# Another written-out order of steps, with casts, copies and state writes moved between engines, in a retention-plus-MLP kernel

## The chip, the core and the metric

The kernel runs on one core of one Trainium2 chip. A core has five engines, each of which works through its own instruction stream in order: TensorE (PE in the profile, with its weight loads as PEld), VectorE (DVE), ScalarE (ACT), GpSimd (POOL) and SyncE (SP). Here SP only issues DMAs, and POOL issues DMAs beside its arithmetic. The metric is the time of the whole program in device microseconds (us). Before the change it is 296.88 us, the median of three runs (296.61 to 297.04).

## The reference, cut to what matters

```python
q, k, v: (8 batches, 8 heads, 576 tokens, 64), float32; w_in (512, 2048); w_out (2048, 512)

scores = q @ k.transpose(0, 1, 3, 2) / sqrt(64)
gamma  = 1 - 2 ** (-5 - head)
Dmat   = gamma ** (row - col) where row >= col, else 0       # a decaying causal mask
x      = ((scores * Dmat) @ v), heads side by side           # (4608 tokens, 512)
h      = x @ w_in
g      = 0.5 * h * (1 + tanh(sqrt(2 / pi) * (h + 0.044715 * h ** 3)))
out    = g @ w_out                                           # (4608, 512)
```

## The kernel before, in words

**Retention.** A batch of 576 tokens is cut into five units: four of 128 tokens and a tail of 64. Units are numbered through, u = 0 to 39; u % 5 = 4 is a tail. Units 0, 2, 5 and 7 stand for two units each ("wide", 256 tokens). The decay is folded into the casts: `q` and `v` are multiplied by powers of gamma while they are cast from float32 to float16, and a running state of 64 by 64 per head carries the past. `L,u,n` loads q, k or v (n = 0, 1, 2) of unit u into one of seven pages of float32 (three from unit 31 on). `q,u`, `k,u`, `v,u` cast; the letter at the end names the engine (v VectorE, g GpSimd, a ScalarE). `D,u` transposes q and k of a unit by one DMA on SP; the first units are transposed on TensorE instead (`t`, copied out by `y`). `B,u,w` is a unit's TensorE work: the scores and the state products of unit u, and the output of unit w, the one before. Wide units have `X`, `Y` and `R` for that. `m,u` masks the scores, `a,u,half` and `o` update the state, `z,u,half` writes it as float16, `x,w` writes the output to xT, the left operand of the MLP. B has one buffer for scores and one for outputs, so the next B needs `m` and `a` of the last unit, and `x` of the one before, to be done.

**MLP.** Tokens go in nine blocks t of 512. For blocks 0 to 5, `N,t,fc,part` multiplies 256 tokens by 256 columns of w_in (eight matmuls), and `F` applies gelu. For blocks 6 to 8 the same product is made in four groups g of seven smaller products each (`A,t,g,i`, four matmuls) from sums of weights (`U`) and sums of xT (`s`); `l` combines them and `f` applies gelu. The second product is plain in block 0 and in the end of block 8 (`O`, four matmuls of 512 columns, copied out by `e`; `P` for the last rows, copied out by `E`). In between it is made in pairs of 128 rows by seven products (`W,t,pr,i`, eight matmuls) from sums of weights (`T`) and sums of gelu outputs (`H`); `V` combines the results, and `S` stores them (`Q` for the last rows). N, A and P share two PSUM banks, and so do O and W.

**Order.** Nothing is scheduled by a planner at run time. `ORDER` lists 1,332 steps, and each engine gets its instructions in the order of that list; the engines wait for each other by semaphores only. What a step is next to in the list means something only on its own engine. A step that waits holds up what stands behind it on that engine: a `D` on SP waits for its two casts, an `S` for its result, and the loads behind them wait too.

**Weights.** `I,g` (w_in) and `J,g` (w_out), eight each, are DMAs that GpSimd issues and that cast on the way; `N` with fc = 0 and 2 needs I,0 and I,1, fc = 4 and 6 needs I,2 and I,3, fc = 8 and 10 needs I,4 and I,5, fc = 12 and 14 needs I,6 and I,7. `O` of part p (the second number modulo 4) needs J,2p and J,2p+1. The steps `i` and `j` do nothing here, since all weights are loaded that way. `K,n` issues n matmuls whose result is not used, to fill TensorE's time before the first work. `w` loads the table of gelu, `c`, `g` and `Z` write constants and zeros.

Lines of the profile: 198 and 203 (wide loads), 215 and 221 (loads; 221 tails), 238 (weights), 269 and 267 (copies and casts on VectorE or GpSimd, and on ScalarE), 424 and 439 (q and v casts, wide ones), 483 (`D`), 529, 553, 563, 574 (`B`), 757 (`N`), 765 (`F`), 775 (`S`), 783 (`O`), 817 (`T`, `H`, `V`, `U`, `s`, `l` as sums), 860 (`W`), 957 (`A`), 987 (`P`), 1003 (`K`).

Of the kernel before, what the change touches and what calls it, by code (L numbers as in the profile page):

```python
# [17 lines left out]
L,0,1 Z,1,v L,0,0 I,2,g L,0,2 L,2,1 L,2,0 Z,2,g q,0 k,0,g I,7,g K,4 K,4 K,4 K,3 K,4 t,0,q,h L,2,2  # L18
L,4,1 c t,0,k,h I,1,g v,0,v X,0 y,0,k,v I,0,g I,3,g a,0,1 y,0,q,v Z,3,v k,2,g K,4 K,1 Y,0,1 t,2,k,o
m,0,1 z,0,1,a I,6,g K,4 Y,0,0 a,1,1 q,2 L,4,0 K,4 t,2,q,h m,0,0 y,2,k,a y,2,q,v I,4,g K,1 R,0 I,5,g  # L20
x,0 Y,2,1 L,5,0 x,1 i,4,v K,3 N,0,2,0 N,0,0,0 g o,1,1 m,2,1 L,5,1 Z,4,g v,2,v F,0,2,0 N,0,12,0 Y,2,0
F,0,0,0 z,1,1,v N,0,4,0 L,5,2 X,2 k,4,g Z,5,v q,4 F,0,12,0 F,0,4,0 t,4,k,o a,2,1 t,4,q,o a,3,1
y,4,q,a N,0,8,0 L,4,2 z,2,1,g L,9,1 N,0,10,0 F,0,8,0 k,5,g m,2,0 L,7,1 R,2 F,0,10,0 y,4,k,v B,4,-1
q,5 x,3 x,2 N,0,14,0 L,7,0 t,5,q,o N,0,0,1 L,7,2 J,1,g F,0,14,0 N,0,6,0 y,5,q,v J,3,g t,5,k,o
F,0,0,1 m,4 j,1,v J,0,g L,9,0 v,5,v J,2,g L,9,2 F,0,6,0 N,0,8,1 L,10,0 N,0,12,1 k,7,v X,5 y,5,k,a
F,0,8,1 z,3,1,g F,0,12,1 v,4,v Y,5,0 a,5,1 m,5,0 a,6,1 N,0,4,1 N,0,6,1 F,0,4,1 q,7 F,0,6,1 t,7,k,o
y,7,k,a N,0,2,1 J,5,g J,4,g N,0,14,1 F,0,2,1 J,6,g L,10,2 B,-1,4 F,0,14,1 x,4 Y,5,1 t,7,q,h y,7,q,a
J,7,g m,5,1 N,0,10,1 v,7,v F,0,10,1 z,5,1,g R,5 x,5 Y,7,0 o,6,1 x,6 O,0,0 O,0,4 q,10,g L,11,1
N,1,4,0 O,0,5 N,1,14,0 F,1,4,0 m,7,0 N,1,2,0 L,12,2 O,0,1 X,7 Y,7,1 F,1,14,0 F,1,2,0 L,15,1 k,9,a
O,0,6 O,0,2 N,1,10,0 F,1,10,0 q,9,g O,0,3 L,11,2 N,1,6,0 D,9 F,1,6,0 m,7,1 Z,0,g k,11,a a,7,1 O,0,7  # L30
e,0,0,v a,8,1 z,6,1,v O,0,12 T,1,0,v N,1,0,0 e,0,1,a F,1,0,0 z,8,1,g z,7,1,v N,1,8,0 O,0,13 L,10,1
N,1,12,0 R,7 B,9,-1 H,1,0,3,v v,10,v F,1,8,0 x,8 O,0,8 L,11,0 L,12,1 O,0,14 j,5,v F,1,12,0 v,11,v
T,1,1,v q,11 k,10,g x,7 O,0,15 N,1,6,1 H,1,0,1,v L,12,0 D,10 N,1,8,1 O,0,9 F,1,6,1 T,2,0,v v,9,v
O,0,10 e,0,3,a T,3,0,v S,0,0 N,1,14,1 F,1,8,1 H,1,0,2,v m,9 L,14,1 B,10,9 k,12,a D,11 T,2,1,v O,0,11
a,10,0 a,10,1 e,0,2,v N,1,12,1 L,13,2 F,1,14,1 L,13,0 x,9 N,1,10,1 m,10 F,1,12,1 T,3,1,v z,10,0,g
B,11,10 q,12,g W,1,0,1 S,0,3 v,13,v a,11,0 V,1,0,0,a a,11,1 x,10 v,12,v W,1,0,6 L,14,0 F,1,10,1
N,1,2,1 o,11,1 q,13,g F,1,2,1 T,4,0,v D,12 W,1,0,2 L,16,1 V,1,0,1,v N,1,4,1 N,1,0,1 S,0,2 V,1,0,2,a
z,11,0,v F,1,4,1 z,10,1,g j,2,v m,11 S,0,1 N,2,0,0 B,12,11 q,14 a,12,0 H,1,0,4,v k,15,g F,1,0,1
F,2,0,0 W,1,0,7 L,15,0 L,14,2 N,2,8,0 T,4,1,v N,2,4,0 V,1,0,3,v H,1,1,1,v L,13,1 z,12,0,g x,11
k,16,g H,1,1,2,v W,1,0,4 W,1,0,5 F,2,8,0 L,17,0 a,12,1 N,2,6,0 L,17,1 V,1,0,5,v L,19,0 F,2,4,0  # L40
k,13,g D,13 V,1,0,4,v F,2,6,0 m,12 N,2,14,0 v,14,v F,2,14,0 W,1,1,1 z,11,1,g V,1,1,0,a W,1,0,3
V,1,0,6,v L,16,0 N,2,10,0 F,2,10,0 k,14,g W,1,1,6 V,1,1,1,v N,2,12,0 z,12,1,v L,16,2 B,13,12 x,12
L,15,2 v,15,g D,14 q,15 W,1,1,2 H,1,1,3,v m,13 N,2,2,1 V,1,1,2,a W,1,1,7 F,2,12,0 N,2,2,0 V,1,1,3,v
k,17,a W,1,1,4 W,1,1,5 a,13,0 a,13,1 S,1,0 z,13,0,a q,19 q,17 q,16 F,2,2,1 S,1,1 D,15 L,17,2 F,2,2,0
L,18,0 N,2,8,1 B,14,13 N,2,12,1 L,20,0 F,2,8,1 V,1,1,5,v F,2,12,1 N,2,6,1 V,1,1,4,v W,2,0,1 x,13
N,2,10,1 F,2,6,1 m,14 H,2,0,1,v H,2,0,2,v z,13,1,v N,2,0,1 D,16 V,2,0,0,a L,24,1 B,15,14 H,1,1,4,v
a,15,0 L,18,2 H,2,0,3,v W,1,1,3 a,15,1 F,2,0,1 m,15 V,1,1,6,v q,18,g v,17,v F,2,10,1 N,2,4,1
N,2,14,1 L,18,1 L,19,1 x,14 v,16,g F,2,14,1 W,2,0,2 z,15,0,g B,16,15 W,2,0,6 F,2,4,1 x,15 k,19,g
a,16,0 N,3,8,0 V,2,0,1,v V,2,0,2,a a,16,1 F,3,8,0 o,16,1 z,16,0,v m,16 W,2,0,7 D,17 V,2,0,3,v L,23,1
v,18,g N,3,10,0 k,18,g F,3,10,0 L,24,0 L,20,1 N,3,4,0 F,3,4,0 z,15,1,g W,2,0,4 z,16,1,v B,17,16  # L50
L,21,0 N,3,0,0 q,20 V,2,0,5,v a,17,0 L,25,1 L,19,2 D,18 H,2,0,4,v L,20,2 S,1,2 W,2,0,5 N,3,12,0
W,2,1,1 F,3,0,0 m,17 q,21,g H,2,1,3,v V,2,0,4,v H,2,1,1,v F,3,12,0 k,20,g W,2,0,3 N,3,14,0 N,3,6,0
S,1,3 F,3,14,0 V,2,0,6,v V,2,1,0,a L,22,1 N,3,2,0 L,21,1 D,19 H,2,1,2,v W,2,1,6 a,17,1 x,16 z,17,0,g
# [73 lines left out]
def kernel(  # L127
# [11 lines left out]
    B, H, S, D = q.shape  # L139
# [239 lines left out]
    for h in range(H):  # L379
        pp, m = divmod(h, 4)  # L380
# [363 lines left out]
    gTs, h = {}, {}  # L744
# [331 lines left out]
```

## Time and profile before

| | us |
|---|---|
| median of three runs | 296.88 (296.61 to 297.04) |
| profiled execution: span from the first to the last instruction | 293.9 |
| profiled execution: its own time apart from the span | not given by the page |
| median less span | 3.0 |
| TensorE busy in the span | 280.3 (95%) |
| VectorE, ScalarE, GpSimd busy | 216.6, 150.1, 109.6 |
| first `N` starts | 21.3 |
| TensorE's last matmul group starts (32 matmuls, 2.65 us) | 288.2 |
| DMAs moved | 49.79 MB; HBM read 36.70 MB, written 9.44 MB |

The granted TensorE clock is full in all 40 slices. A busy TensorE says little by itself, since matmuls overlap and their ends are modelled; so it is read by the spacing of their starts: eight matmuls of 256 columns follow each other in 0.87 us (109 ns each), four of 512 columns in 0.86 us. By this pace the steps of the list can be laid out on a scale of TensorE work, counted from the first `N`: N and W are 0.87 us each, A 0.44, O 0.86, B 0.3 to 0.8. Positions such as "+20.9" below are this count, and "lead" is the distance of two steps on it.

### The profile page before, as it was taken

The page shows a single profiled execution, that of the slowest core. Times are in us where ns is not written, and L with a number is a line of the kernel's source. Part 1 is how long each engine was busy: PE and PEld are TensorE (multiplying, and loading weights), DVE is VectorE, ACT ScalarE, POOL GpSimd, SP SyncE. Part 2 cuts the span into 40 slices and gives each one's busy share as a digit, 9 for nine tenths or more (in the row PEclk, how much of TensorE's full clock was granted, in tenths as well). Part 3 has the DMA queues.
Part 4 walks back from the last instruction along what each step waited for, and adds up shares of the span by engine and source line. Part 5 has one row for each costly group of instructions (what it writes and reads, how often), then busy time and mean ns, then how long its engine had stood idle before and what let it go on. Part 6 is the DMA issues. An engine that isn't in the chain of part 4 may idle for free.

```text
span 293.9 us, 9639 instructions
## 1 busy us (share of the span) xinstructions
PE 280.3 (95%) x4064; PEld 235.2 (80%) x4064; DVE 216.6 (74%) x447; ACT 150.1 (51%) x289; POOL 109.6 (37%) x168
## 2 busy tenths in 40 slices
PE   3797999999999999999999999999999999999995
PEld 1355886667888888888888888888888788888874
DVE  7686753696865678576678699799889988977740
ACT  2144774334634543554553646546777587665411
POOL 5931910414351084163415544783467123000000
PEclk9999999999999999999999999999999999999999
DMA  7999999997979999989099978899498370002103
GB/s 212 283 236 250 217 220 211 214 179 162 248 142 228 178 186 220 230 206 210 23 235 214 196 166 178 187 204 153 131 195 208 75 205 7 36 8 102 74 25 121
DMA packets 136428, 49.79 MB, mean 169 GB/s; under 512 B 118208, under 2 KB 130880, under 8 KB 136384
## 3 DMA queue, kind: packets, MB, share of 16 engines
q1 hardware_dynamic: 132032, 44.97, 71.3%
q0 software_dynamic: 4352, 4.20, 8.5%
q8 instruction: 32, 0.52, 0.8%
q14 instruction: 12, 0.10, 0.1%
HBM read 36.70 MB, written 9.44 MB: 157 GB/s over the span
## 4 chain that ended last, share of the span: by engine, by line
PE 86%; POOL 5%; DMA 4%; DVE 3%; issue 1%; ACT 0%; POOLq 0%; ACTq 0%
PE bank L860 30%; PE bank L757 27%; PE bank L957 12%; PE bank L783 6%; DMA w_in_sb<-in_moe_w_in_dram 4%; PE sk L553 2%; PE x L529 2%; POOL w_in_sb L238 2%; PE sk L563 1%; PE x L574 1%; PE bank L987 1%; DVE pages L817 1%; POOL wide L269 1%; PE bank L493 1%; PE x L677 1%
## 5 line engine op out<-in xcount | busy, mean ns | idle before, releaser
L757 PE MATMUL bank<-xT,w_in_sb 128*128 128x256 f16 x768 | 94.4, 273 | 2.1 <-DMA w_in_sb<-in_moe_w_in_dram 2.1
L765 ACT ACTIVATE gT<-bank 128x512 f16<-128x512 f32 x96 | 56.7, 598 | 61.5 <-PE bank L757 59.7
L757 PEld LDWEIGHTS <-w_in_sb 128*128 128x128 f16 x768 | 73.8, 98 | 13.7 <-DMA w_in_sb<-in_moe_w_in_dram 2.7
L860 PEld LDWEIGHTS <-ssum 128*128 128x128 f16 x480 | 46.3, 98 | 6.5 <-issue 0.8
L269 POOL CAST sz<-s 64x256 f16<-64x256 f32 x48 | 24.4, 509 | 66.2 <-DVE s L713 45.9
L860 PE MATMUL bank<-tsum,ssum 128*128 128x256 f16 x360 | 46.0, 273 | 0.6 <-DVE ost L817 0.6
L860 PEld LDWEIGHTS <-gT 128*128 128x128 f16 x360 | 34.8, 98 | 4.5 <-issue 0.2
L424 POOL TENSOR_TENSOR qk<-pages,dec 128x512 f16<-128x512 f32 (+1 forms) x20 | 22.2, 1122 | 32.9 <-DMA pages<-in_q_dram 17.2
L860 PE MATMUL bank<-w_out_sb,gT 128*128 128x256 f16 x240 | 31.1, 273 | 0.0
L817 DVE TENSOR_TENSOR ssum<-gT 128x1024 f16<-128x1024 f16 x30 | 23.9, 798 | 3.9 <-ACT gT L765 3.5
L424 POOL TENSOR_TENSOR v<-pages,dec 128x512 f16<-128x512 f32 (+1 forms) x20 | 20.6, 1030 | 15.3 <-DMA pages<-in_v_dram 10.4
L817 DVE TENSOR_TENSOR ost<-u,bank 128x256 f32<-128x256 f32 x45 | 18.1, 416 | 9.5 <-PE bank L860 9.4
L817 DVE TENSOR_TENSOR ssum<-gT,ssum 128x1024 f16<-128x1024 f16 x30 | 23.4, 782 | 0.2
L691 DVE TENSOR_TENSOR ret<-sk,mask 128x512 f16<-128x512 f32 (+1 forms) x32 | 19.8, 618 | 4.3 <-PE sk L563 4.0
L957 PEld LDWEIGHTS <-pages 128*128 128x128 f16 x192 | 18.4, 98 | 2.8 <-issue 0.3
L957 PE MATMUL bank<-pages 128*128 128x256 f16 x144 | 20.3, 273 | 0.3 <-ACT pages L267 0.3
L783 PE MATMUL bank<-w_out_sb,gT 128*128 128x512 f16 x80 | 19.1, 380 | 0.0
L817 DVE TENSOR_TENSOR u<-u,bank 128x256 f32<-128x256 f32 x30 | 12.4, 415 | 8.7 <-PE bank L860 5.0
L713 DVE TENSOR_TENSOR s<-s,sk 128x256 f32<-128x256 f32 x36 | 14.9, 415 | 5.0 <-PE sk L563 4.0
L593 ACT ACTIVATE xT<-x 128x512 f16<-128x512 f32 (+1 forms) x25 | 14.3, 578 | 8.0 <-PE x L574 8.0
L817 DVE TENSOR_TENSOR hc<-hc,bank 128x512 f32<-128x512 f32 x21 | 14.4, 684 | 5.0 <-PE bank L957 2.3
L267 ACT COPY hc<-bank 128x512 f32<-128x512 f32 x19 | 11.1, 585 | 12.5 <-PE bank L957 12.4
(114 smaller groups left out, 425.8 us busy)
## 6 DMA issues: line engine op xcount, KB each, us to landing
out_dram<-ost SPq DMA_DIRECT2D x35, 256.0 KB, 3.4
pages<-in_q_dram SPq DMA_DIRECT2D x32, 256.0 KB, 4.7
pages<-in_v_dram SPq DMA_DIRECT2D x24, 256.0 KB, 4.1
pages<-in_k_dram SPq DMA_DIRECT2D x24, 256.0 KB, 4.3
pages<-in_k_dram SPq DMA_DIRECT2D x4, 512.0 KB, 5.2
pages<-in_v_dram SPq DMA_DIRECT2D x4, 512.0 KB, 6.0
w_in_sb<-in_moe_w_in_dram POOLq DMA_DIRECT2D x8, 256.0 KB, 9.8
w_out_sb<-in_moe_w_out_dram POOLq DMA_DIRECT2D x8, 256.0 KB, 10.6
```

The lines of the kernel that those rows point to most:

```text
L267: nc.scalar.copy(out=o, in_=i)
L269: (nc.vector if eng == "v" else nc.gpsimd).tensor_copy(out=o, in_=i)
L424: eng.tensor_tensor(out=out, in0=s["raw"][:, i, 0:n], in1=dec[:, i // 2, s["j"], 0:n].unsqueeze(2).to_broadcast([128, n, D]), op=ALU.mult,)
L593: nc.scalar.activation(out=xT[:, :, o : o + G * (b - a)].rearrange("c p (h s) -> c p h s", s=G), in_=x[:, a:b].rearrange("c h p s -> c p h ...
L691: nc.vector.tensor_tensor(out=ret[:, :, 0:n], in0=now["two"][:, :, 0, 0:n], in1=mask.unsqueeze(1).unsqueeze(1).to_broadcast([128, 2, n, G] ...
L713: nc.vector.tensor_tensor(out=s32, in0=state[0], in1=kv, op=ALU.add)
L757: nc.tensor.matmul(hps[:, i, :], w_in_sb[:, ct, 128 * (fc + i) : 128 * (fc + i) + 128], xT[:, ct, TB * t % XR + lo : TB * t % XR + hi], st ...
L765: nc.scalar.activation(out=gTs[t][:, fc : fc + TB // (hi - lo), lo:hi], in_=h.pop((t, fc, lo)), func=AF.Gelu_apprx_tanh, bias=0.0, scale=1.0,)
L783: nc.tensor.matmul(ops[t, tcc], gTs[t][:, ft, 128 * tcc : 128 * tcc + 128], w_out_sb[:, ft, :], start=(ft == 0), stop=(ft == NFC - 1),)
L817: (nc.vector if eng == "v" else nc.gpsimd).tensor_tensor(out=out, in0=a, in1=b, op=op)
L860: nc.tensor.matmul(p["ps", bank][:, HN * col : HN * col + HN], a[:, k], b[:, k], start=(k == 0 and i in (1, 6)), stop=(k == HK - 1), skip_ ...
L957: nc.tensor.matmul(p["ps", bank][:, n], w[:, c, 128 * n : 128 * n + 128], x[:, c], start=(n == 0 and c == 0 and i in (1, 2, 5)), stop=(c = ...
```

## The change

The 1,332 steps stay the same, one for one, except that 125 of them name another engine, and all are put in another order. Of the 125: 16 `z` go from GpSimd to ScalarE, 8 from GpSimd to VectorE, 12 to GpSimd (5 from ScalarE, 7 from VectorE), 5 from VectorE to ScalarE, 2 from ScalarE to VectorE; 12 `V` go from ScalarE to VectorE; 10 `q` go to GpSimd and 8 to VectorE; 9 `v` go to VectorE and 6 to GpSimd; 22 `k` change among three engines; 6 `l`, 4 `y`, 3 `e`, one `E` and one `Z` change. By the rows' durations, ScalarE gets some 9 us more, GpSimd 10.6 us less and VectorE 1.3 us more.

At the start, the DMAs of I,0, I,7 and I,1 come first on GpSimd, `g` and `w` come early, and SP loads q of unit 2 first. The pair's four buffers are chosen by the pair's number in the block and no longer by a running count; both lists open the pairs in the order (1,0), (1,1), (2,0) and so on, so the buffers come out the same.

```diff
 ORDER = """
-L,0,1 Z,1,v L,0,0 I,2,g L,0,2 L,2,1 L,2,0 Z,2,g q,0 k,0,g I,7,g K,4 K,4 K,4 K,3 K,4 t,0,q,h L,2,2
-L,4,1 c t,0,k,h I,1,g v,0,v X,0 y,0,k,v I,0,g I,3,g a,0,1 y,0,q,v Z,3,v k,2,g K,4 K,1 Y,0,1 t,2,k,o
-m,0,1 z,0,1,a I,6,g K,4 Y,0,0 a,1,1 q,2 L,4,0 K,4 t,2,q,h m,0,0 y,2,k,a y,2,q,v I,4,g K,1 R,0 I,5,g
-x,0 Y,2,1 L,5,0 x,1 i,4,v K,3 N,0,2,0 N,0,0,0 g o,1,1 m,2,1 L,5,1 Z,4,g v,2,v F,0,2,0 N,0,12,0 Y,2,0
...
-T,1,1,v q,11 k,10,g x,7 O,0,15 N,1,6,1 H,1,0,1,v L,12,0 D,10 N,1,8,1 O,0,9 F,1,6,1 T,2,0,v v,9,v
-O,0,10 e,0,3,a T,3,0,v S,0,0 N,1,14,1 F,1,8,1 H,1,0,2,v m,9 L,14,1 B,10,9 k,12,a D,11 T,2,1,v O,0,11
...
+I,0,g K,4 I,7,g K,4 K,4 Z,1,v K,4 K,1 K,3 I,1,g L,2,0 K,3 g L,0,0 c q,0 t,0,q,h L,0,1 w k,0,v L,0,2
+t,0,k,h I,3,g v,0,v y,0,k,v X,0 L,2,1 y,0,q,a a,0,1 a,1,1 Y,0,1 I,2,g K,4 m,0,1 k,2,g Y,0,0 m,0,0
+z,0,1,a t,2,k,o I,6,g q,2,g t,2,q,h y,2,q,v R,0 I,4,g K,4 Z,0,g K,1 y,2,k,a Y,2,1 Z,2,g Z,3,v K,4
+j,7,g L,2,2 o,1,1 z,1,1,g x,1 x,0 N,0,2,0 L,4,1 Z,4,g N,0,0,0 v,2,v X,2 m,2,1 L,4,0 Y,2,0 I,5,g
+Z,5,g a,2,1 a,3,1 z,2,1,g F,0,2,0 N,0,4,0 z,3,1,g F,0,0,0 N,0,12,0 F,0,4,0 F,0,12,0 m,2,0 k,4,v R,2
+x,2 x,3 q,4 L,5,0 q,5,g L,4,2 N,0,14,0 F,0,14,0 N,0,6,0 F,0,6,0 L,5,1 t,4,k,o y,4,k,v N,0,12,1
+F,0,12,1 N,0,0,1 t,4,q,o y,4,q,v J,0,g k,5,v N,0,8,1 F,0,0,1 F,0,8,1 N,0,8,0 F,0,8,0 B,4,-1 m,4
+L,5,2 v,5,v t,5,q,o y,5,q,a N,0,6,1 F,0,6,1 t,5,k,o y,5,k,a J,1,g N,0,2,1 F,0,2,1 N,0,10,0 F,0,10,0
+J,5,g v,4,g X,5 a,5,1 z,5,1,a L,7,0 q,7,g a,6,1 i,6,v Y,5,0 m,5,0 N,0,14,1 F,0,14,1 N,0,4,1 F,0,4,1
+B,-1,4 x,4 Y,5,1 L,7,1 t,7,q,h y,7,q,a k,7,g t,7,k,o N,0,10,1 F,0,10,1 L,7,2 L,9,1 m,5,1 R,5 y,7,k,v
+Y,7,0 m,7,0 O,0,4 O,0,0 x,6 x,5 N,1,0,0 F,1,0,0 N,1,10,0 J,3,g L,9,0 N,1,8,0 v,7,v F,1,10,0 j,0,v
+X,7 o,6,1 a,7,1 Y,7,1 J,2,g a,8,1 q,9 k,9,a D,9 z,8,1,v L,10,0 N,1,6,0 F,1,8,0 J,4,g T,1,0,v T,2,0,v
+F,1,6,0 N,1,4,0 O,0,5 F,1,4,0 O,0,1 z,7,1,v J,7,g N,1,12,0 z,6,1,v F,1,12,0 N,1,2,0 L,10,1 F,1,2,0
+O,0,6 J,6,g q,10,g N,1,14,0 F,1,14,0 H,1,0,1,v O,0,7 e,0,1,a O,0,2 O,0,3 m,7,1 R,7 j,3,a T,3,1,v x,7
+L,14,1 e,0,0,a L,11,1 T,4,0,v B,9,-1 O,0,8 O,0,9 O,0,10 L,12,0 x,8 N,1,8,1 O,0,11 N,1,0,1 L,10,2
+T,1,1,v T,2,1,v T,4,1,v k,10,g v,10,v e,0,2,v D,10 F,1,8,1 L,9,2 N,1,2,1 i,7,v v,9,g m,9 B,10,9 m,10
...
+x,30 L,33,0 a,31,0 N,5,2,1 z,31,0,a W,4,1,7 i,0,a L,33,1 q,32,g L,35,0 s,6,1 a,31,1 s,6,2 W,4,1,6
+V,4,1,1,v V,4,1,3,v S,4,0 N,5,12,1 F,5,2,1 F,5,12,1 s,6,3 s,6,4 A,6,0,1 l,6,0,0,a D,32 L,35,1
+W,4,1,5 H,5,0,3,v W,4,1,4 k,34,a L,37,1 H,5,0,4,v k,33,g V,4,1,4,v L,33,2 z,30,1,a A,6,0,6 L,35,2
...
+V,8,0,4,v W,8,0,3 V,8,0,5,v V,8,0,6,v S,8,0 O,8,8 O,8,9 f,8,3,3 f,8,2,3 P,2 E,2,v O,8,10 S,8,1
+O,8,11 e,8,2,v S,8,2 P,0 E,0,a Q,0 P,1 E,1,a Q,2 Q,1
...
-            n = len(pairs)
-            pairs[t, pr] = dict(s=[ssum[4 * (n % 2) + i] for i in range(4)])
+            pairs[t, pr] = dict(s=[ssum[4 * pr + i] for i in range(4)])
```

## The prediction

> **What bounds the kernel now.** The page comes first: engines, then slices.
>
> ```profile
> PE 280.3 (95%) x4064; PEld 235.2 (80%) x4064; DVE 216.6 (74%) x447; ACT 150.1 (51%) x289; POOL 109.6 (37%) x168
> PE   3797999999999999999999999999999999999995
> DVE  7686753696865678576678699799889988977740
> DMA  7999999997979999989099978899498370002103
> ```
>
> TensorE is short of work in the first four slices only. DMA is full for some 130 us, VectorE nearly full in the last third. The waits of TensorE say what its idle time was for:
>
> ```profile
> PE bank L1003 <- DVE ident L364: 4.5, 1, 4.5
> PE bank L757 <- DMA w_in_sb<-in_moe_w_in_dram: 2.1, 2, 1.6
> PE bank L1003 <- DVE qkT L269: 1.9, 1, 1.9
> PE bank L860 <- DVE ost L817: 0.6, 1, 0.6
> PE bank L957 <- DVE pages L817: 0.4, 1, 0.4
> ```
>
> The 4.5 and the 1.9 lie before the first `N`. After it, 2.1 us are w_in arriving late, and 1.0 us VectorE being late at 226 to 229 us. TensorE's timeline, early:
>
> ```profile
> 21.30 1.91 PE L757 MATMUL bank<-xT,w_in_sb 128*128 128x256 f16 x16
> 24.85 1.05 PE L757 MATMUL bank<-xT,w_in_sb 128*128 128x256 f16 x8 [1.64 <-DMA w_in_sb<-in_moe_w_in_dram]
> 28.61 1.70 PE L757 MATMUL bank<-xT,w_in_sb 128*128 128x256 f16 x14 [0.46 <-DMA w_in_sb<-in_moe_w_in_dram]
> ```
>
> So the work proper starts at 21.30, and from there the time is TensorE's work plus these few waits. The pace of the steps proves it: the first `O` starts at 44.31, 23.0 us after the first `N`; the list has 20.9 us of TensorE work between them, and 2.1 us are the two waits. What an order can gain is thus the start, 2.1, 1.0, and little else; what it can lose has no such limit. Two views show where transfers are tight, the weights' landing and SP's timeline:
>
> ```profile
> L238 POOL DMA_DIRECT2D w_in_sb<-in_moe_w_in_dram x8: 713/724/899, 6.4 to 15.8; - x8
> DMA to landing us min/median/max: 6.7/9.8/12.8
> ```
>
> ```profile
> 32.22 4.71 SPq L221 DMA_DIRECT2D pages<-in_q_dram  x2
> 53.69 1.68 SPq L483 DMA_TRANSPOSE qkT<-qk  x1
> 64.58 1.25 SPq L483 DMA_TRANSPOSE qkT<-qk  x1
> ```
>
> Of the weights, the first needs 6.7 us from issue; with others ahead, each lands about 1.85 us after the one before (the last two were issued at 15.05 and 15.76 and landed 26.7 and 28.6). SP's lines are L,9,0, D,9 and D,10.
>
> **The change, part by part.** *Start.* Today q of unit 0 lands at 6.8 (two DMAs issued at 1.30 and 1.97, landing in 4.3 to 4.8) and v at 8.6. The new list loads q of unit 2 first; by the same bytes, q lands near 7.0, k 8.7, v 10.5 to 11.5 (three weights are now in flight from 6.4). VectorE: q 1.2, k 0.94, v 1.25, the copy of kT 1.2, the two state steps 0.8, to 14.3; mask, scores, mask 1.2 each with 0.4 between, to 17.3. GpSimd: three weights from 6.43 to 8.8, `c` 1.45, two weights, k of unit 2 at 13.5 to 14.5, one weight, q of unit 2 to 17.5. No row has a wide q on GpSimd; 128x512 takes 1.04 to 1.12, so twice that, 2.2 (bounds 1.2, VectorE's, and 3). R,0 can run at 17.5 to 18.3, against 18.71 before. Behind it stand K, Y,2,1, K: first `N` at 20.5. Gain 0.8, between 2 and -1. `g` (1.25) falls to VectorE before q lands, `w` (1.28) to ScalarE before it has work: both at nothing; without that cover they would cost their own length. The index of the buffers and the steps `i`, `j` change nothing.
>
> *w_in.* Eight issues on GpSimd, now at about 6.4, 7.3, 8.0, 10.3, 11.0, 14.5, 17.5 and, behind `z,1,1` which waits for `o`, 21.4. With 6.7 us for a first one and 1.85 for the next, they land at 13.1, 15.0, 16.9, 18.7, 20.6, 22.4, 24.3, 28.1. Needed: I,1 (third) at 20.5, I,2 (fifth) at 23.0, I,6 (sixth) at 23.9, I,5 (last) at 30.0, 9.5 us of work after the first `N`. All are in time: the 2.1 us go. Next in line is I,5 with 1.9 us to spare. Bounds: 0 and -2.1.
>
> *w_out.* J,0, J,1, J,5 are issued near 28 to 30; then GpSimd waits for q of unit 7, so J,3, J,2, J,4, J,7, J,6 come at 37 to 40. Landing by the same rule: 44.0, 45.9, 47.7, 49.6, 51.4; needed by `O` at +27.8, +31.2, +33.0, which is 48.3, 51.7, 53.5. Two us to spare: 0, at most +2.
>
> *SP at unit 9.* Today L,9,0 is issued at 32.2 and D,9 runs at 53.69, with seven loads issued between. The new list puts D,9 directly behind L,9,0, so SP stands still until that load lands (15.2 to 16.2 us after issue: 48) and its cast is done; L,10,0 and all that follows, D,10 and L,9,2 among them, come after D,9. D,9 at 49.7 + 1.5; six loads of 0.6; D,10 waits for two casts on GpSimd, to 58.9; L,9,2 to 60.3, landed (3.8) at 63.5, cast (0.65) at 64.2. Its reader, the last part of B,10,9, stands at +42.6 and 0.5 more: 63.6. Loss 0.6; if D,9 comes 2 us earlier none, 2 us later 2.6. I take 0.5.
>
> *Engines.* VectorE has 1.3 us more in all, ScalarE 9 more (16 `z` of 0.83), GpSimd 10.6 less. On GpSimd a `z` waits long for its state, and holds up the casts behind it:
>
> ```profile
> POOL sz L269 <- DVE s L713: 45.9, 9, 8.4
> ```
>
> On ScalarE the same wait holds up `F`, `l` and `x`, for which TensorE's next N, A and B wait. ScalarE is busy for 13.6 to 14.5 of 20 us at most, so I set this at 0; where a `z` stands ahead of an `F` with a bank to free, each costs up to its 0.83. The 12 `V` cost VectorE 0.41 each, in place of 0.37 on ScalarE. VectorE is the risk:
>
> ```profile
> 200.00:220.00 20.00, 20.00 (x346) 17.86 (x345) 17.22 (x37) 14.54 (x29) 9.54 (x14) 1.00 0.76 155
> 220.00:240.00 20.00, 18.95 (x265) 16.45 (x263) 19.32 (x37) 13.57 (x28) 8.45 (x11) 1.00 0.68 159
> ```
>
> Its busy time (third figure behind the stretch's length) is 97% where the 1.0 us was lost. By the rows' durations, 165 to 180 us after the first `N` had 19.5 us of VectorE steps in 15 us of TensorE work; the new list has 18.8 and 15.8 in the two stretches 150 to 180, so the queue is longest where `A` starts and its banks turn over every 0.44 us. Between +193 and +204, where the loss was, it has less. I take +0.7 for the one (from 0 to +4) and -0.4 for the other (-1.0 to 0).
>
> *Transposing DMAs.* In the list 9 of 31 have under 1 us of TensorE work to the `B` that reads them; before, 4. Landing takes 3.3 to 3.9. SP runs ahead of TensorE, so this costs nothing where the casts are early; the late one is unit 39, whose k load stands behind D,38 and whose cast stands in VectorE's queue: 0, up to +1.5.
>
> *End.* Q,2 now stands between Q,0 and Q,1; one issue takes 0.33 to 0.45: +0.35. The last copies change engine at equal length (0.42 and 0.37).
>
> Sum: -0.8 - 2.1 + 0.5 + 0.7 - 0.4 + 0.35 = -1.75. The profiled span 293.94 becomes 292.2; the runs' median stands 2.94 above that span (the execution's own time is not given), so 295.1.
>
> *A rule on VectorE and GpSimd.* Sums of gelu outputs read two tensors and take 0.68 while GpSimd is idle, but 1.13 at 103.27 beside a GpSimd cast and 1.42 here:
>
> ```profile
> 226.25 1.42 DVE L817 TENSOR_TENSOR ssum<-gT,ssum 128x1024 f16<-128x1024 f16 x1
> ```
>
> The Trainium skill, "SBUF — State Buffer", section "Who interferes with whom", says that a VectorE instruction with two SBUF inputs contends with a GpSimd instruction that reads SBUF. The trace agrees in these rows. By that rule, less GpSimd work shortens VectorE's queue: the 60 sums last 0.79 on average, 0.11 over the undisturbed, 6.6 us in all, and a tenth less GpSimd work gives 0.66 back. The sum without it stands.
>
> **The rivals.** *SP's head of line (slower).* The mechanism at unit 9, larger: each us that D,9 runs after 49.1 is lost at B,10,9, and the loads behind it come late for units 10 to 12 too. For it: seven of the nine loads of units 9 to 11 stand at most 6.3 us of TensorE work ahead of their cast; before, six of them stood 9 to 32 us ahead. Against: with nothing else issued, L,9,0 should land sooner. At 53.69, D,9's old time, it costs 4.6 in place of 0.5: 299.2; from 51.4 on it outweighs all gains.
>
> *VectorE's queue at the first `A` (slower).* At 4 us in place of 0.7: 298.4. For it: the load above. Against: the old list had as much at +135 to +150 and lost nothing there.
>
> *No gain at the start (no change).* If weights land by bytes, since DMA is full, I,6 lands at 24.8 as today and the 2.1 stay: 297.2. Against: loads wanted later than today do not crowd it.
>
> *All waits go (faster).* Terms for SP and VectorE at 0, the 1.0 gone entirely: 293.3; with the shorter VectorE sums of the rule, 292.6.
>
> **How the numbers follow.** The forecast, 294 to 296.2, has 0.44; all waits gone 0.11; no gain at the start 0.12; SP 0.18; VectorE 0.15. A measurement of this kernel can tell 0.2% (0.6 us) from no change. The first two are faster, 0.55; the third is split 0.09 no change and 0.03 slower; of SP's and VectorE's 0.33 a small part, 0.03, ends within 0.2%: no change 0.12, slower 0.33. The range for 8 in 10 reaches from within the waits-gone case, 292.8, to SP's case, 299.2; the forecast's own is 294 to 296.2.
>
> **What would show it.** Right: first `N` near 20.5, no wait of L757 for w_in, first `O` near 41.4. D,9's start and the last L574 of B,10,9 (63.6) decide on SP: L553 or L574 idle on GpSimd's v. Idle time of L957 or L860 on L817 between 185 and 215 us decides on VectorE. Wrong: any TensorE wait over 1 us elsewhere, above all after 60 us, which I have not followed step by step.

## The result, and the profile after

The changed kernel takes 303.79 us (median of four runs, 303.32 to 306.18); the kernel before took 296.75 beside it (four runs, 296.18 to 297.04). The ratio is 1.0253, with a 95% interval of 1.0212 to 1.0294: 7 us slower, where 1.8 us faster was forecast.

The page of the changed kernel, engines and slices:

```profile
PE 282.7 (94%) x4064; PEld 236.9 (78%) x4064; DVE 219.3 (73%) x452; ACT 160.3 (53%) x308; POOL 95.0 (31%) x144
PE   4928989999999999999998999899999999999995
DVE  7625377655747677685689798999888898877741
PEclk9987999999999999999999999999999999999999
```

The engines' totals moved as foreseen in sign: ScalarE 10.2 us more, GpSimd 14.6 less, VectorE 2.7 more. The loss stands in slices 3 and 4 (15 to 30 us): TensorE has a 2 and an 8 there, VectorE a 2 and a 5, and the granted clock, which the page of before gives as full in every slice, falls to 0.8 and 0.7. The waits of TensorE:

```profile
PE bank L493 <- POOL wide L269: 4.9, 1, 4.9
PE bank L1002 <- DVE ident L364: 4.5, 1, 4.5
PE bank L493 <- POOL wide L439: 1.6, 1, 1.6
PE bank L493 <- DVE wide L269: 1.2, 1, 1.2
PE bank L859 <- DVE u L817: 0.9, 1, 0.9
PE x L529 <- ACT sz L267: 0.9, 1, 0.9
```

The 2.1 us for w_in are gone, as forecast. At the top stands a wait that did not exist before: the transposes of unit 2 (L493) wait 4.9 us for its k and 1.6 for its q, both cast on GpSimd. TensorE's timeline shows who pays (rows between 25.21 and 28.99 left out):

```profile
21.21 1.03 PE L493 MATMUL bank<-ident,wide 128*128 128x128 f16 x8 [4.89 <-POOL wide L269]
23.82 1.03 PE L493 MATMUL bank<-ident,wide 128*128 128x128 f16 x8 [1.57 <-POOL wide L439]
25.21 1.07 PE L677 MATMUL x<-ret_wide,wide 64*64 64x128 f16 x32
28.99 1.91 PE L757 MATMUL bank<-xT,w_in_sb 128*128 128x256 f16 x16
```

The first `N` starts at 28.99, against 21.30 before and 20.5 forecast. From there on nothing is lost in sum: to the last `P` it is 266.7 us in both kernels (the last `P` of before starts at 288.05, not at the 288.2 given above). So nearly the whole result is the first 29 us. SP's timeline, and GpSimd's with the issues of the weights and the cast of k:

```profile
0.80 2.59 SPq L198 DMA_DIRECT2D pages<-in_q_dram  x4
3.44 0.59 SPq L203 DMA_DIRECT2D pages<-in_k_dram  x1
4.70 3.09 SPq L203 DMA_DIRECT2D pages<-in_k_dram  x1
```

```profile
6.44 2.33 POOL L238 DMA_DIRECT2D w_in_sb<-in_moe_w_in_dram  x3
10.18 1.51 POOL L238 DMA_DIRECT2D w_in_sb<-in_moe_w_in_dram  x2
20.13 1.03 POOL L269 CAST wide<-pages 128x1024 f16<-128x1024 f32 x1 [8.44 <-DMA pages<-in_k_dram]
```

The load issued at 4.70 is k of unit 2. Its size and its time from issue to landing, in the kernel before and in the changed kernel:

```profile
pages<-in_k_dram SPq DMA_DIRECT2D x1, 512.0 KB, 7.1
pages<-in_k_dram SPq DMA_DIRECT2D x1, 512.0 KB, 15.3
```

So it lands at 20.0, 15.3 us after its issue; before it was issued at 3.27 and landed at 10.4. Two things were new around it: two loads of q at the head of SP's list, and three weights issued at once from 6.44 on. Which of them, whether TensorE's order of transposes or the clock has its own share, and what the later waits are, the experiments decide.

### The profile page after: what moved, and what is told of

It reads as the page before. It is cut to its first block, busy times and chain, and to the rows that moved or that the text cites. A ratio compares the mean times of both kernels' runs of the same rounds, so it can differ in the third digit from the quotient of the medians.

```text
span 301.8 us, 9629 instructions
## 1 busy us (share of the span) xinstructions
PE 282.7 (94%) x4064; PEld 236.9 (78%) x4064; DVE 219.3 (73%) x452; ACT 160.3 (53%) x308; POOL 95.0 (31%) x144
## 5 line engine op out<-in xcount | busy, mean ns | idle before, releaser
L757 PE MATMUL bank<-xT,w_in_sb 128*128 128x256 f16 x768 | 94.1, 273 | 0.0
L757 PEld LDWEIGHTS <-w_in_sb 128*128 128x128 f16 x768 | 73.4, 98 | 10.6
L424 POOL TENSOR_TENSOR qk<-pages,dec 128x512 f16<-128x512 f32 (+1 forms) x19 | 20.3, 1074 | 31.5 <-DMA pages<-in_q_dram 19.9
L424 POOL TENSOR_TENSOR v<-pages,dec 128x512 f16<-128x512 f32 (+1 forms) x17 | 17.1, 1004 | 34.8 <-DMA pages<-in_v_dram 20.5
L817 DVE TENSOR_TENSOR ost<-u,bank 128x256 f32<-128x256 f32 x45 | 18.5, 416 | 11.6 <-PE bank L859 11.3
L269 POOL CAST qk<-pages 128x512 f16<-128x512 f32 (+1 forms) x17 | 12.2, 719 | 33.3 <-PE bank L757 10.2
L817 DVE TENSOR_TENSOR ssum<-gT,ssum 128x1024 f16<-128x1024 f16 x30 | 21.2, 707 | 0.3
L267 ACT CAST sz<-s 64x256 f16<-64x256 f32 x44 | 17.7, 402 | 5.0 <-DVE s L713 2.2
L269 POOL CAST sz<-s 64x256 f16<-64x256 f32 x20 | 8.8, 441 | 31.5 <-DVE s L713 23.3
```

The costliest lines, as they stand in the source:

```text
L267: nc.scalar.copy(out=o, in_=i)
L269: (nc.vector if eng == "v" else nc.gpsimd).tensor_copy(out=o, in_=i)
L424: eng.tensor_tensor(out=out, in0=s["raw"][:, i, 0:n], in1=dec[:, i // 2, s["j"], 0:n].unsqueeze(2).to_broadcast([128, n, D]), op=ALU.mult,)
L757: nc.tensor.matmul(hps[:, i, :], w_in_sb[:, ct, 128 * (fc + i) : 128 * (fc + i) + 128], xT[:, ct, TB * t % XR + lo : TB * t % XR + hi], st ...
L817: (nc.vector if eng == "v" else nc.gpsimd).tensor_tensor(out=out, in0=a, in1=b, op=op)
```

## The experiments

Theory W is that the early weights crowd out k of unit 2; theory H, which grew out of the first runs, that they can do so only because two loads of q at the head have cost the DMA engines their first microseconds. The rivals are SP's order as such (S, F), TensorE's order (Q) and the clock (C).

**Three weights later.**

```diff
-I,0,g K,4 I,7,g K,4 K,4 Z,1,v K,4 K,1 K,3 I,1,g L,2,0 K,3 g
+I,0,g K,4 K,4 K,4 Z,1,v K,4 K,1 K,3 I,1,g L,2,0 K,3 g
...
-t,0,k,h I,3,g v,0,v
+t,0,k,h v,0,v
...
-Y,0,1 I,2,g K,4 m,0,1 k,2,g Y,0,0
+Y,0,1 K,4 m,0,1 k,2,g I,7,g I,3,g I,2,g Y,0,0
```

> The changed list with three of the five early weights (I,7, I,3, I,2) issued behind the cast of k of unit 2 on GpSimd; nothing else moved. Theory W (bytes): weights and loads share the DMA engines, and k of unit 2 lands at 20.0 us because five weights and four other loads are in flight with it. In the profile of before the eight weights took 41.3% of sixteen engines' 30 us, so 1.55 us each. Then k of unit 2 lands 3 x 1.55 = 4.6 us sooner, at 15.4, the first N starts near 24.4 in place of 29.0, and the time is near 299, less if the granted clock stays full, more if the three weights are now late for N. Rival S (place in SP's list): k of unit 2 is late because it is the fifth load and not the fourth; then it lands at 19 to 20 as now, and the time stays at 303.8.

Measured: 301.92 us (300.75 to 302.58), ratio 1.0165 (1.0122 to 1.0208). k of unit 2 landed at 16.1, 3.9 us sooner, near W's 4.6. But the first `N` came at 28.48. GpSimd now spent 2.9 us on four weight issues between the two casts of unit 2, so q of unit 2 was ready at 22.0; and the granted clock was 0.5 from 18 to 28 us, so that the five `K` before Y,2,1 took 2.32 us; they take 1.25 at full clock (in the run with unit 2's loads exchanged) and took 1.62 in the changed kernel. W is right about the landing, and the landing alone does not make the start.

**q and k of unit 2 exchanged in SP's list.**

```diff
-K,3 I,1,g L,2,0 K,3 g L,0,0 c q,0 t,0,q,h L,0,1
+K,3 I,1,g L,2,1 K,3 g L,0,0 c q,0 t,0,q,h L,0,1
...
-y,0,k,v X,0 L,2,1 y,0,q,a
+y,0,k,v X,0 L,2,0 y,0,q,a
```

> The changed list with L,2,0 and L,2,1 exchanged: k of unit 2 is loaded first, q of unit 2 fifth. Theory W: whatever is loaded fifth lands near 20; k's cast goes early, but q of unit 2 takes its place, its cast ends near 22, t,2,q at 23, and R,0 stands behind it: first N near 27.5, time 302.3. Rival S: k of unit 2 alone is what holds the start; then the first N comes at 20.5 to 22 and the time is 295 to 297.

Measured: 295.30 us (292.73 to 298.51), ratio 0.9941 (0.9908 to 0.9974): faster than before. First `N` at 20.16. W as I had put it is refuted: q of unit 2, now fifth, did not land at 20. Its cast began at 13.85 without a wait. So a load of as many bytes, in the same place of the list, beside the same weights, landed at least 6 us sooner. The edit changes two things at once, though: the fifth load is now q, and the load at the head is now k. (The profiled execution of this run is the slowest of its ten, 298.5 us: 2.0 us went at 40 us, where k of unit 7 came late, and the clock was halved behind that wait.)

**R,0 and the first `N` ahead of unit 2's transposes.**

```diff
-z,0,1,a t,2,k,o I,6,g q,2,g t,2,q,h y,2,q,v R,0 I,4,g K,4 Z,0,g K,1 y,2,k,a Y,2,1 Z,2,g
+z,0,1,a I,6,g q,2,g R,0 I,4,g K,4 Z,0,g K,1 Z,2,g
...
-Z,4,g N,0,0,0 v,2,v
+Z,4,g N,0,0,0 t,2,k,o t,2,q,h y,2,q,v y,2,k,a Y,2,1 v,2,v
```

> The changed list with the transposes of unit 2 (t,2,k, t,2,q, their copies and Y,2,1) moved behind N,0,0,0, so that R,0 and the first two N do not stand behind them on TensorE. Theory Q (TensorE's order): R,0 needs nothing of unit 2 and could run from 17.5; the first N then starts at 20.5 to 21.5. The casts of unit 2 still hold up GpSimd to 20 and 24, so I,6, I,4 and I,5 are issued as late as now (21.1, 23.7, 29) and land 6.7 us later: N with fc = 12 waits some 2.5 us for I,6 and the transposes of unit 2 wait 2 us: time 298 to 300. Rival: R,0 itself is held by v of unit 0 or by the mask; then the first N stays at 27 to 29 and the time at 302 to 304.

Measured: 302.38 us (301.20 to 303.20), ratio 1.0191 (1.0151 to 1.0231). The first `N` started at 20.07, so R,0 had indeed only stood behind unit 2. Almost nothing came of it: between 22 and 28 us TensorE waited 1.60 us at the transposes of q of unit 2, for a bank that a gelu still held, and 1.31, 0.72 and 0.49 for the copies, the cast and the mask of unit 2, and the granted clock was 0.5 to 0.7 from 26 to 34, so that sixteen matmuls of `N` took 3.60 us in place of 1.91. In this order the late landing was paid further on; other places for the transposes were not tried.

**The start of before, the rest of the changed list.** The steps up to N,0,0,0 are those of the list before, on its engines; the others follow in the changed order.

> The steps up to N,0,0,0 in the order and on the engines of before, the rest in the order of the changed list. If all of the loss is in the start: first N at 21.3, the 2.1 us of waits for w_in come back, and from the first N on 272.8 + 2.1: span 296.2, time 298 to 298.5. If the new start only pays for something that comes later (rival: the early weights save more than 2.1 us further on), the waits behind the first N are 4 us or more and the time is 300 or over.

Measured: 295.40 us (293.34 to 296.22), ratio 0.9950 (0.9923 to 0.9977). First `N` at 21.77, and from there 270.1 us in the profile against 272.6 before and 272.8 in the changed kernel. So the whole loss lies in the start, and the rest of the changed list is in this profile even a little better than the old one. The 2.1 us for w_in that I expected back did not come.

**k of unit 0 at the head.** One load is moved; k of unit 2 stays fifth, the weights stay early.

```diff
-K,3 I,1,g L,2,0 K,3 g L,0,0 c q,0 t,0,q,h L,0,1 w
+K,3 I,1,g L,0,1 L,2,0 K,3 g L,0,0 c q,0 t,0,q,h w
```

> The changed list with k of unit 0 (L,0,1) moved to the head of SP's loads; k of unit 2 stays the fifth load, and the weights stay as early as they are. Theory H (the head): with two loads of q first the DMA engines are only 81 to 85% busy from 4 to 8 us (over 100% in before), so that some 250 KB less have been moved by 8 us and k of unit 2 falls into the time in which the weights share the engines; a load of k at the head fills them, k of unit 2 lands by 13.5, the first N starts at 20 to 21.5, time 294.5 to 296.5. Rival F (fifth place): with the same four loads ahead of it, k of unit 2 lands at 18 to 20 as now, the first N starts at 27 to 29, time 302 to 304.

Measured: 293.89 us (291.99 to 298.09), ratio 0.9907 (0.9874 to 0.9941), the best run of all. H holds, F falls. SP's and GpSimd's timelines of this run:

```profile
0.80 0.45 SPq L199 DMA_DIRECT2D pages<-in_k_dram  x1
1.31 2.57 SPq L194 DMA_DIRECT2D pages<-in_q_dram  x4
4.56 0.58 SPq L199 DMA_DIRECT2D pages<-in_k_dram  x1
```

```profile
6.44 2.32 POOL L234 DMA_DIRECT2D w_in_sb<-in_moe_w_in_dram  x3
12.11 1.03 POOL L265 CAST wide<-pages 128x1024 f16<-128x1024 f32 x1
```

and the first `N` on TensorE:

```profile
19.63 1.91 PE L753 MATMUL bank<-xT,w_in_sb 128*128 128x256 f16 x16
```

(Lines of these runs are numbered four lower.) The weights are issued at the same 6.44, the fifth load at 4.56 in place of 4.70, and its cast begins at 12.11 without waiting for a transfer, 8.0 us sooner than in the changed kernel. What differs is how full the DMA engines were in between, by stretch, this run first and then the changed kernel:

```profile
4.00:8.00 4.00, 3.49 (x9) 1.29 (x10) 2.89 (x27) 1.93 (x4) 3.04 (x8) 1.00 1.06 363
```

```profile
4.00:8.00 4.00, 3.49 (x9) 1.29 (x10) 3.44 (x28) 1.93 (x4) 3.04 (x8) 1.00 0.83 247
```

The last two figures are the DMA engines' share and GB/s. What SP's queue had moved by 10 us (packets, MB, share of the engines): this run, the kernel before, the changed kernel, and the run with unit 2's loads exchanged:

```profile
q1 hardware_dynamic: 3326, 2.44, 79.0%
q1 hardware_dynamic: 3531, 2.33, 82.1%
q1 hardware_dynamic: 2554, 2.05, 69.0%
q1 hardware_dynamic: 3518, 2.31, 81.3%
```

Five loads are 2.62 MB: here 0.18 MB, a third of k of unit 2, is left when the weights begin to move; in the changed kernel 0.57, all of it. What that means is shown by the DMA queues while both have work. The same three figures for the changed kernel at 14 to 17 us:

```profile
q0 software_dynamic: 443, 0.43, 83.7%
q1 hardware_dynamic: 446, 0.22, 36.0%
```

and the run with unit 2's loads exchanged, at 11 to 14:

```profile
q0 software_dynamic: 394, 0.37, 73.7%
q1 hardware_dynamic: 376, 0.37, 43.3%
```

q0 carries the weights, q1 SP's loads. While both have work, the profile counts about as many packets of the one as of the other: 443 and 446, 394 and 376. A packet of a weight has 0.97 KB, one of k or v 0.5 KB, one of q up to 2 KB. So loads of k and v get 0.22 of 0.65 MB in 3 us beside weights, and the 1,024 packets of one take 6.9 us; with q among them it is 0.37 MB. At 0.073 MB per us the 0.57 MB left at 10 us would have landed near 17.8, by this estimate; k of unit 2 landed at 20.0, and SP's queue moved 0.91 MB from 10 to 20 us, so later loads moved beside its last packets. What held them back is open.

Two things therefore parted the run with unit 2's loads exchanged from the changed kernel: with k at its head less was left at 10 us (0.31 MB), and what was left was q, in larger packets. The two were not tried apart. k in the fifth place is harmless when little of it is left, as this run shows. The Trainium skill, "DMA: Bandwidth & Descriptors", section "Queues, rings and completion order", says that each DMA engine takes turns between the queues that have work for it, by packets and not by bytes. The equal counts agree. Whether a turn is one of the profile's packets or several, they don't show; the page has typically 9 to 17 descriptors in a packet, and the profile's packet may be a smaller thing.

**Matmuls in the gap.** 22 more matmuls without use, 16 ahead of t,2,k and 6 ahead of t,2,q.

```diff
-z,0,1,a t,2,k,o I,6,g q,2,g t,2,q,h
+z,0,1,a K,16 t,2,k,o I,6,g q,2,g K,6 t,2,q,h
```

> The changed list with 22 more matmuls whose result is not used, 16 ahead of t,2,k and 6 ahead of t,2,q, where TensorE stands idle for 4.9 and 1.6 us. Theory C (clock): TensorE's idle time is followed by a granted clock of 0.5 from 20 to 27 us, which makes t,2,q, R,0 and the K behind it take 5.2 us from 23.8 on in place of 3.9; with the idle time filled the clock stays full, the first N starts near 27.7 in place of 29.0, and the time is near 302.5. Rival: the clock falls whatever TensorE does, or the filling itself delays the transposes: first N at 29 to 30, time 303.5 to 305.

Measured: 299.96 us (298.52 to 301.38), ratio 1.0108 (1.0067 to 1.0150). C holds: the gain is 3.8 us by the medians, where 1.3 was its price, but not all of it is the clock. The same stretch in the changed kernel and in this run (third from the end: the granted clock):

```profile
24.00:26.00 2.00, 2.00 (x44) 1.80 (x42) 1.11 (x1) 0.00 (x0) 1.46 (x3) 0.50 1.10 210
```

```profile
24.00:26.00 2.00, 2.00 (x55) 1.13 (x53) 2.00 (x4) 1.09 (x2) 1.07 (x3) 1.00 1.21 247
```

First `N` at 26.98, 2.0 us sooner: 0.6 of it because k of unit 2 happened to land sooner (cast at 19.53), which leaves some 1.4 for the clock, about its price. The other 1.1 us between the two profiles lie behind the first `N` (271.7 us against 272.8), and the filling doesn't explain them; the four runs of each kernel spread over 3 us. The mean clock over the run, 0.977 to 0.989 in the changed kernel's four executions, is 0.993 to 1.0 in this run's.

**Casts of unit 5 back to their old engines.**

```diff
-q,5,g
+q,5
...
-k,5,v
+k,5,g
```

> The changed list with only two casts given back the engines of before: q of unit 5 to VectorE, k of unit 5 to GpSimd. Theory P (two engines at one port): the cast of k of unit 5 takes 4.27 us on VectorE because GpSimd runs a wide product and two casts beside it, and TensorE waits 1.2 us for it; given back, the wait is gone and the time falls by 0.8 to 1.2, to 302.6 to 303. Rival: the cast is long because its data lands late, and the transposes wait for k of unit 5 anyway: the wait stays at 1 us or more and the time at 303.8.

Measured: 301.34 us (299.02 to 303.12), ratio 1.0151 (1.0081 to 1.0221). The wait is gone. From the first `N` on the profile has 271.3 us in place of 272.8; the rest of the gain is k of unit 2, which happened to land at 17.1 here.

**The cast of k of unit 5 left where it is, its neighbour moved.**

```diff
-X,5 a,5,1 z,5,1,a L,7,0 q,7,g a,6,1
+X,5 a,5,1 z,5,1,a L,7,0 q,7 a,6,1
```

> The changed list with one cast moved: q of unit 7 from GpSimd to VectorE, so that the cast of k of unit 5 on VectorE has only two shorter casts of GpSimd near it. Theory P (one port): the cast of 128x1024, 0.75 to 0.94 us alone and 4.27 beside GpSimd's row of three, falls below 2.5 us though it is unchanged itself, and TensorE's wait of 1.2 us for it goes: time lower by 1 or so, near 302.5. Rival: the cast is slow for its own operands or place: it stays above 4 us.

Measured: 302.48 us (300.60 to 304.46), ratio 1.0174 (1.0121 to 1.0227). The cast on VectorE, in the changed kernel with GpSimd's instructions beside it, and then in this run:

```profile
38.44 4.27 DVE L269 CAST wide<-pages 128x1024 f16<-128x1024 f32 x1
```

```profile
38.68 0.65 POOL L424 TENSOR_TENSOR v<-pages,dec 128x256 f16<-128x256 f32 x1
39.25 1.92 POOL L439 TENSOR_TENSOR wide<-pages,decw 128x1024 f16<-128x1024 f32 x1
41.10 1.05 POOL L269 CAST wide<-pages 128x1024 f16<-128x1024 f32 x1
```

```profile
39.34 0.75 DVE L265 CAST wide<-pages 128x1024 f16<-128x1024 f32 x1
```

The GpSimd product beside it in this run:

```profile
39.59 0.96 POOL L420 TENSOR_TENSOR v<-pages,dec 128x256 f16<-128x256 f32 x1
```

P holds for the cast: the same instruction takes 4.27 us beside three GpSimd instructions in a row and 0.75 without the long one among them, and the 1.2 us wait goes. The run with filling matmuls has the slow one again, 4.32. The run's time does not show the gain: from the first `N` on this profile has 272.4 us against 272.8, since other waits came. The Trainium skill, "SBUF — State Buffer", "Who interferes with whom", which the prediction used for instructions with two inputs, says in its next point that casts and copies in VectorE's two-port mode and GpSimd shut each other out entirely, and that whoever issues first keeps the shared port. The trace agrees that a cast, with its one input, is shut out. On who wins it doesn't settle the matter: in this run the cast, recorded 0.25 us ahead of the GpSimd product, ran through, and the product took 0.96 in place of 0.65; in the changed kernel the cast is recorded from 38.44 on, 0.24 us ahead of the first of the three, and ends after the last.

**The engines of before, the order of the changed list**, from N,0,0,0 on (121 steps differ).

> The changed list in its own order, but from N,0,0,0 on every step on the engine that it has in before (121 steps differ; V, z, q, k, v, l). Theory V (VectorE's queue): the 2.7 us that TensorE idles between 160 and 220 us in the changed kernel come from the 12 V and the casts that moved to VectorE; then the idle time there falls below 1 us, the 1.2 us at unit 5 go too, and the time is near 300.5. Rival O (the order alone): W and A stand too close to the sums they read whatever engine does the rest; the idle time stays at 2 us or more, and the time at 302.5 or over, more if z on GpSimd is late.

Measured: 340.49 us (338.70 to 343.52), ratio 1.1495 (1.1419 to 1.1571). Both theories missed by far. TensorE waits 8.9 us for transposing DMAs of q and k and 2.9 for state writes on GpSimd, and is idle for 1.5 to 5 us in most stretches of 20. An order and its choice of engines belong together; what one of the two is worth alone can't be read from such a run.

**k of unit 0 at the head, and two sums later.**

```diff
-q,28 U,1,0 F,4,6,1 L,31,0 W,3,1,7 V,3,1,3,v N,4,12,1
+q,28 F,4,6,1 L,31,0 W,3,1,7 V,3,1,3,v N,4,12,1
...
-V,3,1,4,v W,3,1,4 V,3,1,5,v N,4,10,1
+V,3,1,4,v W,3,1,4 V,3,1,5,v U,1,0 N,4,10,1
...
-W,4,1,2 x,28 U,4,0 H,4,1,3,v L,34,0 B,30,29
+W,4,1,2 x,28 H,4,1,3,v L,34,0 B,30,29
...
-a,30,0 k,32,a N,5,0,1 a,30,1 v,32,v
+a,30,0 k,32,a N,5,0,1 a,30,1 U,4,0 v,32,v
```

> The changed list with k of unit 0 at the head of SP's loads, and two of the sums of w_in later on VectorE: U,4,0 behind the state sums of unit 30 (a,30,1) in place of ahead of them, U,1,0 behind V,3,1,5. Theory V (VectorE's queue): the run with k of unit 0 first still idles TensorE 0.80 us at 156 (a W whose banks wait for V behind U,1,0) and 0.81 + 0.45 us at 187 (B of units 31 and 30, whose state write on ScalarE waits for the state sums, which stand behind a sum of gelu outputs of 1.43 and U,4,0 of 1.53 us). With the two sums later both waits shrink by 0.7 to 0.8 each: 292.3 to 292.8, against 293.9. Rival: the long sums only move the lateness to the next step of the queue: 293.5 to 294.2.

Measured: 293.91 us (292.57 to 295.81), ratio 0.9916 (0.9887 to 0.9946): no difference from the run without the second edit. The waits of 0.80 and 0.81 us went; for the mask (L687) on VectorE TensorE waited 1.01 at 160 us, which is new, and 0.62 at 188, where it was 0.45. From 150 to 205 us the waits for VectorE are 1.63 us in place of 2.58, so part of the loss moved and part went. Against that the first `N` came at 20.17, with a wait of 0.38 for w_in behind it, and k of unit 7 cost 1.09 at 40 us. The medians show no gain, as the rival has it; that an order only chooses which step is late is not shown, since the runs of each of the two spread over 3 us and more.

**The two parts of the start, one at a time, in the kernel before.** First only the order of the five loads, then only the places of the five weights.

```diff
-L,0,1 Z,1,v L,0,0 I,2,g L,0,2 L,2,1 L,2,0 Z,2,g q,0 k,0,g
+L,2,0 L,0,0 L,0,1 L,0,2 L,2,1 Z,1,v I,2,g Z,2,g q,0 k,0,g
```

> The kernel before with only SP's first five loads in the order of the changed list: q of unit 2, q, k and v of unit 0, k of unit 2. The weights stay at their later places. Theory H (the head of SP's loads): with two loads of q first, k of unit 0 lands near 9.8 in place of 4.9 and k of unit 2 at 14 to 15 in place of 10.4; the first N starts at 23 to 25 and the time is 298.5 to 300. Rival E (the early weights alone do it): the loads' order costs nothing where no more weights are in flight than before: 296 to 297.5.

Measured: 297.42 us (296.60 to 299.12), ratio 1.0020 (1.0001 to 1.0038). First `N` at 23.36, as H expected; the time is 1 us better than it expected, since the waits for w_in fell from 2.1 to 0.5 at the same time: the first `N`, 2.1 us later, gave the weights time.

```diff
-L,0,1 Z,1,v L,0,0 I,2,g L,0,2 L,2,1 L,2,0 Z,2,g q,0 k,0,g I,7,g K,4
+I,0,g I,7,g I,1,g L,0,1 Z,1,v L,0,0 L,0,2 L,2,1 L,2,0 Z,2,g q,0 k,0,g K,4
...
-L,4,1 c t,0,k,h I,1,g v,0,v X,0 y,0,k,v I,0,g I,3,g a,0,1
+L,4,1 c I,3,g I,2,g t,0,k,h v,0,v X,0 y,0,k,v a,0,1
```

> The kernel before with only the five weights on GpSimd as in the changed list: I,0, I,7, I,1 first, I,3 and I,2 behind the constants. SP's loads stay as they are, k of unit 0 first. Theory H: k of unit 2 has landed by 11 us, when the weights begin to take their share; the first N stays at 21 to 21.5 and the 2.1 us of waits for w_in become 0 to 0.5, as the prediction had it: 294.5 to 295.5. Rival E (early weights crowd out k of unit 2 whatever comes first): k of unit 2 lands at 15 or later, the first N starts at 24 or later, time 298 or more.

Measured: 295.89 us (294.61 to 296.74), ratio 0.9961 (0.9942 to 0.9980). k of unit 2 was cast at 13.49 without waiting for its transfer, and the waits for w_in went. The gain is 1 us and not 2, because the first `N` came at 22.28: the clock was 0.5 to 0.64 from 14 to 18 us here.

So in the kernel before, the new order of loads alone costs 0.6 us and the early weights alone gain 1.0. In the changed list, where both are present, putting one load of k at the head takes back 9.9 us by the medians, and exchanging unit 2's loads 8.5. Neither part alone does the harm in the kernel before, and in the changed list either of these two changes to the loads removes it. Three weights later took back 1.9 only, with four issues between the casts and a halved clock of its own. A run with both parts in the kernel before was not made, so that it takes both is argued and not shown. Nor was the cast of q of unit 2 moved back alone: it stands on GpSimd behind k's, 1.91 us long, and TensorE waits 1.57 for it.

## Why the prediction was wrong, point by point

**The start failed**, and in one sentence: "k of unit 2 at 13.5 to 14.5". It landed at 20.0. The working counted the loads "by the same bytes" and noted that "three weights are now in flight", but gave the load of k no loss from them. This one landing, with the halved clock behind it, put the first `N` at 28.99 in place of 20.5, 8.5 of the 8.7 us by which the forecast missed. Two things were missing: with q of unit 2 and q of unit 0 at the head the DMA engines were at 83% from 4 to 8 us (106% with k of unit 0 ahead of them), and beside weights a load of k gets only a third of the bytes that move. The other landings were near enough (k of unit 0 forecast 8.7, measured 9.8; v 10.5 to 11.5, measured 11.3), the wide q on GpSimd took 1.91 (2.2 forecast). "R,0 can run at 17.5 to 18.3" was right for the data it needs, as the run with R,0 first shows (17.55), and overlooked that R,0 stands behind the transposes on TensorE. The bound of 1 us for a loss came from no row, and should have come from the spread of landings: 1.85 us for each of three weights is 5.5. Nor was the clock in the sum; the page of before gives it as full, and 4.9 us of idle time were not expected.

**The rivals**: the dearest, 299.2, fell short, and none stood in the right place. "No gain at the start" named the cause, "weights land by bytes, since DMA is full", and applied it to the weights only, not to the load that shared the engines with them.

**w_in**: right. No wait of L757 is left. The late start helped: the last three weights were issued 7.9 and 5.3 us ahead of the first `N` and with it, where 6.0 and 3.0 ahead and 0.9 behind were forecast. But the run with k of unit 0 at the head, with its first `N` at 19.63, has no wait for w_in either; with two sums later besides, and the first `N` at 20.17, it is 0.38. **w_out**: right, no wait. **SP at unit 9**: 0.5 was forecast; D,9 ran at 57.39, which is 28.4 us after the first `N` (29.2 forecast), and B,10,9 did not wait: 0. **Transposing DMAs**: right, no wait for them. **End**: +0.35 forecast; from the last `P` to the end it is 6.1 us in place of 5.9.

**Engines**: too small. "I set this at 0" for ScalarE: a state write on it made a B wait 0.91 us, the price named there (0.83), with the state sums behind VectorE's long sums as the reason. For VectorE the sum had +0.7 and -0.4. The 1.06 us of waits for it before (0.42, 0.64), and 0.29 for ScalarE beside them, went altogether; 1.22 at unit 5, 0.93 at a W, 0.45 at a mask and 0.38 at an A came. All later waits together, with those for w_in before and ScalarE's 0.91 now, are 3.89 us against 3.45, so from the first `N` on nothing was gained. The stretch that was shown of before now reads:

```profile
200.00:220.00 20.00, 19.62 (x277) 17.42 (x276) 17.81 (x38) 11.51 (x24) 8.23 (x11) 1.00 0.91 169
```

VectorE is 89% busy there and the loss 0.4; since the first `N` came 7.7 us later, the stretch holds somewhat earlier work than before's. Most waits came elsewhere, at 43, 166 and 196 us. **The rule on the port** gave 0.66 us of shorter sums; the sixty sums took 45.7 us in place of 47.3. The dearer effect on the port was one that the prediction didn't price: a cast with one input that took 4.27 us in place of 0.75.

**The sum's base**: median less span was 2.94 because the profiled execution of before was a quick one. In the changed kernel an execution lasts 1.7 us longer than its span, so before's profiled one took about 295.6. The forecast span of 292.2 is what the run with k of unit 0 at the head has (292.3), partly by chance: its first `N` is at 19.63 and its later waits are larger than in the sum.

## What to carry to other kernels

Before weights are issued earlier, ask which loads are still unfinished when their packets begin to move, and how large the packets of each are: here both queues moved equal numbers of packets, and the load with the smaller ones got a third of the bytes. An engine that works in order pays for a late operand at whatever stands behind it, and a gap on TensorE can be paid a second time by the clock. Moving one load to the head of a queue was worth 9.9 us here by the medians; the whole changed list with it gains 2.8 on the kernel before.

## What the runs showed that I had not expected

- Weights begin to move 3 to 4 us after their issue (issued 6.44; 4 packets before 9.5 and 43 in the half microsecond from there in the changed kernel, the first 20 in that from 10.0 with k of unit 0 at the head), so what SP's queue had finished by 9.5 us was all but out of their way.
- With q at the head, SP's transfers fall to 184 GB/s from 5.5 to 6.5 us, after the q and before the k behind it; with k at the head they stay at 365 to 373 in the same time. A load of k issued at 0.80 is at full rate from 3.5 on, 2.7 us later; behind q such a time may show as a hole. That is a reading of the rows; why q leaves the engines part idle was not tried.
- A gap halves the granted clock in one run and not in another. The kernel before idles from 12 to 14 us (0.43 us busy) at full clock in its profile; the run with only the early weights, with 0.39 us busy there, had 0.5 from 14 to 16. The Trainium skill, "TensorE: Matmul & The Clock Gate", Part 1, describes a gate that looks at windows of some 3.4 us that run freely, which would explain why one run and not the other. That the clock falls after an idle window of that length, as it says there, would not: here a gap of 1.87 us was enough in one run. The lengths agree with the window, being once, twice and three times that: the clock was halved for 3.4 us in the two runs of the kernel before with a part of the new start, 6.8 in the changed kernel and 10.2 with three weights later. Beyond that the runs show only that gaps of 1.9 to 4.9 us can do it, and that filling the gap of 4.9 prevented it.
